# Sliding-window attention into a hard-swish MLP on one core: q and k of the first three batches loaded as fp32 runs in the queue of v and transposed on TensorE, the diagonal ALiBi and mask of two batches added by matmul, weights loaded a slice at a time

## The chip, the core and the metric

One Trainium2 chip, one of its cores. The core has TensorE (PE, matmuls; its weight loads are PEld), VectorE (DVE), ScalarE (ACT), GpSimd (POOL) and SyncE (SP), which run their own instruction streams and meet at semaphores, and 16 DMA engines that move data between device memory and the on-chip SBUF. Matmuls write to PSUM. The metric is the device time of one execution in microseconds (us).

## What is computed

The inputs q, k, v have 8 batches, 8 heads, 576 positions and 64 numbers per head, in fp32. The attention looks back at most 127 positions and adds a bias that falls linearly with the distance (ALiBi); its output, 4608 tokens of 512 numbers, goes through two weight matrices with a hard-swish between them.

```python
    scores = scale * np.matmul(q, k.transpose(0, 1, 3, 2))
    bias = slopes[:, None, None] * (-np.abs(rel).astype(np.float32))[None, :, :]
    mask = (rel >= 0) & (rel < window)          # rel = query position - key position, window = 128
    scores = np.where(mask, scores + bias[None], -1000000000.0)
    ...                                          # softmax over the keys, times v
    h = x @ w_in                                 # x: 4608 x 512, w_in: 512 x 2048
    g = h * np.clip(h + 3.0, 0.0, 6.0) / 6.0
    return (g @ w_out).astype(np.float32)        # w_out: 2048 x 512
```

## The kernel before

**Pairs and slots.** The attention goes over 32 pairs g = 0 to 31; pair g is two heads (e = 0, 1) of batch b = g // 4, with hp = g % 4. The code is written out in order by hand: each engine runs its instructions as they stand, and nothing is reordered. A *slot* g is what one pass of the loop in `first_batch` (g = 0 to 3) or `segment` (g = 4 to 32) issues.

**One pair.** The window is 128, so a block of 128 queries meets its own block of keys (the diagonal, PSUM tile `scd`, five blocks of which the short fifth lies in `sco[448:512]`) and the block before it (off-diagonal, PSUM tile `sco`). `scores` (L203 to L214) makes both on PE with keys on the partitions. `exp_diag` and `exp_off` (L223, L233, L236) take the exponential on ACT into `pd`, `po` and `p4buf`; the ALiBi bias is ACT's bias per partition (`bias_d`, `bias_o`). The causal and window masks are put on afterwards, by `affine_select` on POOL (L226, L242, L246) or, for `po` of batch 0, by a multiplication on DVE (L239). `values` (L263, L266) multiplies with v, whose 65th column of ones gives the softmax sum, and DVE divides (L271, L272) into `avs`. `back` transposes `avs` into `xT`, either on PE with a copy out of PSUM (L292, L294; batches 0 and 1 and pair 31) or by a transposing DMA (L285, `by_xbar`).

**Where q and k come from.** scores needs q and k with the head dimension on the partitions (`qTb`, `kTb`, two buffers each by batch). Batches 0 and 1 are loaded as *runs*: six consecutive tokens of one head are 1536 contiguous bytes, on 96 partitions. These loads go through POOL's DMA queue (L101), which casts to bf16 on the way; `prepare` (L179) reorders a pair, `transposes` (L191, L193) turns it on PE. From batch 2 on q and k are loaded as *tokens* through SP's queue (L110, pieces of 256 bytes), cast by POOL into the one buffer `tbuf` (L164), and turned by a transposing DMA of SP (`xbar`, L169) that takes a whole batch of q or k. v is always loaded as tokens and cast by POOL into `vbuf` (L157, L160). Four load buffers `ldbuf` are handed from tensor to tensor by `slot_of`. The DMAs of SP take turns on eight semaphores, so that each waits for the one issued eight before it.

**The MLP.** 288 *units* follow the attention: `moe_up` (L303, four matmuls of 512 columns, then ACT L307 and DVE L308) and `moe_down` (L320, four matmuls; every fourth one copies out and stores, L332 to L335). A unit of nt (512 tokens) may only run when the batches that it reads are done (`done`). `fill(n)` puts the next n allowed units at its place; the list of seven numbers per slot says how many stand where. Slots 4 to 7 hold four units each, later ones eight. Units of nt = 0 (16) run from slot 4 to slot 8, those that mix nt = 1 with nt = 0 (32) until slot 12, and from slot 13 on 32 units follow each batch; 80 are left after slot 32. Weights come through POOL's queue with a cast to bf16, each matrix in four slices (L138, L144).

## Time and profile before

| | |
|---|---|
| median of 3 runs | 383.64 us (383.27 to 384.53) |
| the profiled execution, its own time | 384.78 us |
| span of its trace, first to last instruction | 383.1 us |
| busy in the span: PE, ACT, DVE, POOL | 319.5, 200.8, 172.6, 152.1 us |

The span is what the rows below add up to; the profiled execution's time is 1.7 us longer than its span and 1.1 us above the median. A share of busy time is a mean over stages that are limited by different things, so the rows are read by stage.

### The profile page before, as it was taken

Reading aid. Unit: us, or ns where it says so; the run is one execution under the profiler, and the core shown is the slowest. Engines: PE = TensorE matmul, PEld = TensorE weight load, DVE = VectorE, ACT = ScalarE, POOL = GpSimd, SP = SyncE. Lnnn points to the kernel's source line nnn. Section 1 sums busy time; section 2 is a strip of 40 time slices with the busy share of each in tenths; the row PEclk is TensorE's granted clock in tenths of the full one; section 3 lists DMA queues with packets and bytes.
Section 4 is the critical chain, followed back from the end, with each engine's and each line's share of the span. In section 5 each row is a group of like instructions: output and inputs, shape, how many; then the busy total and the mean of one; then the engine's idle time right before and its main releaser. Section 6 shows DMA issues by size and latency. Waiting matters only on the chain.

```text
span 383.1 us, 6502 instructions
## 1 busy us (share of the span) xinstructions
PE 319.5 (83%) x2409; PEld 161.6 (42%) x2445; DVE 172.6 (45%) x357; ACT 200.8 (52%) x365; POOL 152.1 (40%) x265
## 2 busy tenths in 40 slices
...
GB/s 169 196 209 204 184 72 68 169 202 216 206 97 230 163 188 113 227 207 161 201 213 240 143 212 220 150 116 72 46 45 47 45 46 38 27 47 36 27 56 82
DMA packets 153135, 51.64 MB, mean 135 GB/s; under 512 B 141200, under 2 KB 148624, under 8 KB 153104
## 3 DMA queue, kind: packets, MB, share of 16 engines
...
q10 hardware_dynamic: 144, 0.13, 0.1%
...
## 4 chain that ended last, share of the span: by engine, by line
PE 57%; issue 6%; DMA 5%; ACT 5%; POOL 4%; SPq 4%; DVE 4%; POOLq 0%
PE ops L320 27%; PE hps L303 24%; SPq L110 4%; DMA xT<-avs 4%; ACT r L307 3%; POOL pd L226 2%; DVE g L308 2%; PE scd L203 2%; PE av L266 1%; POOL tbuf L164 1%; DMA ldbuf<-in_q_dram 1%; PE av L263 1%; DVE osb L334 1%; POOL po L242 1%; PE sco L210 1%
## 5 line engine op out<-in xcount | busy, mean ns | idle before, releaser
L307 ACT ACTIVATE r<-hps,bias 128x512 f32<-128x512 f32 x144 | 99.7, 692 | 132.0 <-PE hps L303 129.6
L308 DVE SCALAR_TENSOR_TENSOR g<-r,hps 128x512 bf16<-128x512 f32 x144 | 99.0, 687 | 148.7 <-ACT r L307 148.6
L303 PE MATMUL hps<-xT,w_in_sb 128*128 128x512 bf16 x553 | 153.1, 394 | 9.9 <-DMA xT<-avs 5.3
L320 PE MATMUL ops<-w_out_sb,g 128*128 128x512 bf16 x563 | 145.1, 382 | 5.7 <-DVE osb L334 3.9
L320 PEld LDWEIGHTS <-g 128*128 128x128 bf16 x576 | 56.0, 98 | 78.6 <-issue 15.0
L303 PEld LDWEIGHTS <-w_in_sb 128*128 128x128 bf16 x576 | 53.3, 101 | 60.4 <-issue 12.5
L226 POOL TENSOR_SCALAR_AFFINE_SELECT pd<-pd 128x512 bf16<-128x512 bf16 x64 | 39.3, 635 | 60.5 <-ACT pd L223 59.4
L164 POOL CAST tbuf<-ldbuf 128x512 bf16<-128x512 f32 (+1 forms) x60 | 34.3, 613 | 46.5 <-issue 32.7
L233 ACT ACTIVATE po<-sco,bias_o 128x512 bf16<-128x512 f32 x64 | 44.4, 694 | 0.0
L242 POOL TENSOR_SCALAR_AFFINE_SELECT po<-po 128x512 bf16<-128x512 bf16 x56 | 35.4, 639 | 20.4 <-ACT po L233 18.0
L223 ACT ACTIVATE pd<-scd,bias_d 128x512 bf16<-128x512 f32 x64 | 41.1, 685 | 2.3 <-PE scd L203 2.3
L266 PE MATMUL av<-vbuf,pd 128*128 128x65 bf16 x248 | 25.2, 203 | 14.1 <-POOL pd L226 14.1
L266 PEld LDWEIGHTS <-pd 128*128 128x128 bf16 x256 | 21.1, 104 | 24.5 <-POOL pd L226 15.3
L272 DVE TENSOR_TENSOR avs<-av,rc 128x384 bf16<-128x384 f32 (+1 forms) x60 | 29.7, 495 | 2.1
L263 PE MATMUL av<-vbuf,po 128*128 128x65 bf16 x240 | 24.5, 200 | 5.2 <-DVE avs L272 3.6
L263 PEld LDWEIGHTS <-po 128*128 128x128 bf16 x256 | 20.8, 104 | 11.0 <-DVE avs L272 5.6
L271 DVE RECIPROCAL rc<-av 128x6 f32<-128x6 f32 (+1 forms) x60 | 11.0, 183 | 25.9 <-PE av L266 25.9
L157 POOL CAST vbuf<-ldbuf 128x1024 bf16<-128x1024 f32 x16 | 16.3, 1043 | 12.9 <-DMA ldbuf<-in_v_dram 12.9
L236 ACT ACTIVATE p4buf<-sco,bias_d 128x64 bf16<-128x64 f32 x64 | 21.0, 329 | 0.0
L332 ACT COPY osb<-ops 128x512 f32<-128x512 f32 x18 | 10.6, 587 | 19.3 <-PE ops L320 19.3
L191 PE MATMUL tp<-ident,pr 96*128 96x96 bf16 x96 | 8.7, 260 | 11.4 <-DVE pr L179 7.9
L292 PE MATMUL tb<-ident,avs 128*128 128x128 bf16 x45 | 7.0, 270 | 11.0 <-DVE avs L272 10.8
...
## 6 DMA issues: line engine op xcount, KB each, us to landing
...
w_in_sb<-in_moe_w_in_dram POOLq DMA_DIRECT2D x4, 512.0 KB, 11.6
w_out_sb<-in_moe_w_out_dram POOLq DMA_DIRECT2D x4, 512.0 KB, 11.9
...
```

The lines of the kernel that those rows point to most:

```text
L164: nc.gpsimd.tensor_copy(out=tbuf[:m, :, j, :], in_=s[:m, j, :, :].rearrange("p (i e) d -> p i (e d)", e=2))
L223: nc.scalar.activation(out=pd[:, e, :, :].rearrange("p j c -> p (j c)"), in_=sc[:, e, :], func=ACT.Exp, bias=bias_d[:, h:h + 1], scale=scale)
L226: nc.gpsimd.affine_select(out=pd[:, e, :, :], in_=pd[:, e, :, :], pattern=[[0, 4], [1, 128]], channel_multiplier=-1, base=0, compare_op=AL ...
L233: nc.scalar.activation(out=po[:, e, :, :].rearrange("p j c -> p (j c)"), in_=sc[:, e, :], func=ACT.Exp, bias=bias_o[:, h:h + 1], scale=scale)
L242: nc.gpsimd.affine_select(out=po[:, e, :, :], in_=po[:, e, :, :], pattern=[[0, 4], [-1, 128]], channel_multiplier=1, base=-1, compare_op=A ...
L263: nc.tensor.matmul(av[:, i, e, :], lhsT=po[:, e, qt - 1, :], rhs=vb[:, qt - 1, h, :], start=True, stop=False)
L266: nc.tensor.matmul(av[:, i, e, :], lhsT=d, rhs=vb[:, qt, h, :], start=(qt == 0), stop=True)
L272: nc.vector.tensor_tensor(out=st[g, "avs"][:, qts[0]:qts[0] + nq, :, :], in0=av[:, 0:nq, :, 0:D], in1=rc[:, 0:nq, :, :].to_broadcast([128, ...
L303: nc.tensor.matmul(hps, lhsT=w_in_sb[:, ks, ts(ms, 128)], rhs=xT[:, ks, ts(nt, NT)], start=(ks == 0), stop=(ks == n_ks - 1))
L307: nc.scalar.activation(out=r6, in_=hps, func=ACT.Relu, bias=bias3[:, 0:1], scale=1.0 / 6.0)
L308: nc.vector.scalar_tensor_tensor(out=gts[nt][:, ms, :], in0=r6, scalar=1.0, in1=hps, op0=ALU.min, op1=ALU.mult)
L320: nc.tensor.matmul(ops[nt, sub], lhsT=gts[nt][:, ms, ts(sub, 128)], rhs=w_out_sb[:, ms, :], start=(ms == 0), stop=(ms == n_ms - 1))
```

## The change

It does nine things.

1. `NB_PE` is 3: q and k of batch 2 too are loaded as runs and transposed on PE, and `back` transposes batch 2 on PE.
2. The runs go through SP's queue (`load_pair`, a pair at a time, fp32 without a cast; the very first k through ACT's queue), in one order with v's tokens: pairs 0 and 1, v of batch 0, pairs 2 and 3, and from there each pair's runs are loaded when `prepare` of the pair four before has read the buffer.
3. `prepare` therefore casts from fp32. For batch 0 q is done on DVE, k on POOL (k of pair 0 on ACT); for batches 1 and 2 both are on POOL.
4. A table `tab` holds, for each head, the ALiBi term by key position and -2^30 (times the slope) where the mask of the diagonal cuts. For batches 0 and 1 (`NB_TAB`) a matmul with the identity puts it into `scd` and `sco[448:512]` first, and q·k is added to it. One exponential of 1024 columns then makes `pd`, one of 128 makes `p4buf`, and POOL's masks on these two are gone in those slots. The mask on `po` is on POOL in all batches.
5. `scores` now issues the short block in `sco` ahead of `scd`.
6. v of batch 0 is cast in slot 1, five pieces on DVE and POOL; the constants are split into what is needed first and later.
7. The weights' eight slices are issued one per slot (slots 1 and 3 to 9).
8. The first loop now runs to slot 4, `back` in it stands one slot later, and the MLP's units begin with two at the end of slot 4; slots 5 to 8 hold 4, 4, 3 and 3 units. Tokens of batch 3 are loaded from slot 4 on.
9. `by_xbar` leaves out the last pair of each batch from batch 3 on, which `back` transposes on PE.

```diff
-    NB_PE = 2
+    NB_PE = 3
+    NB_TAB = 2
...
+    runs = {nm: ldbuf[slot_of(0, nm)][:RP, :].rearrange("p (h c) -> p h c", h=H) for nm in "qk"}
+
+    def load_pair(g, other=None):
+        b, hp = divmod(g, NP)
+        hs = slice(2 * hp, 2 * hp + 2)
+        for nm, eng in (("q", nc.sync), ("k", other or nc.sync)):
+            eng.dma_start(out=runs[nm][:, hs, :],
+                          in_=src_of[nm][b, hs, :, :].rearrange("h (p t) d -> p h (t d)", t=RT))
...
+        base_i, base_b = base[:, 0:128].bitcast(INT32), base[:, 256:320].bitcast(BF16)
+        nc.gpsimd.iota(base_i, pattern=[[0, 128]], base=-64, channel_multiplier=1)
+        nc.gpsimd.tensor_copy(out=base_b, in_=base_i)
+        nc.gpsimd.affine_select(out=base_b, in_=base_b, pattern=[[1, 128]],
+                                channel_multiplier=-1, base=0,
+                                compare_op=ALU.is_ge, fill=-(2.0 ** 30))
+        for h in range(H):
+            nc.vector.tensor_scalar(out=tab[:, h, :], in0=base_b, scalar1=slopes[h] / scale,
+                                    scalar2=0.0, op0=ALU.mult, op1=ALU.add)
...
+    def load_w_in(g):
+        nc.gpsimd.dma_start(
+            out=w_in_sb[:, :, ts(g, 512)],
+            in_=moe_w_in[:, ts(g, 512)].rearrange("(k p) f -> p k f", p=128))
...
+    def cast_v(b, j, eng):
+        n = min(128, S - j * 128)
+        eng.tensor_copy(out=vbuf[b % 2][:n, j, :, 0:D], in_=ld[b, "v"][:n, j, :, :])
...
-        for nm, eng in (("q", nc.vector), ("k", nc.gpsimd if 2 <= g < NP else nc.vector)):
+        for nm in "qk":
             pr = prs.tile([RP, RT, 2, D], BF16, tag=f"pr{nm}", name="pr")
-            eng.tensor_copy(
-                out=pr.rearrange("p t e d -> p e t d"),
-                in_=ld[b, nm][:, hs, :].rearrange("p e (t d) -> p e t d", t=RT))
+            if g == 0 and nm == "k":
+                copy = nc.scalar.copy
+            elif nm == "q" and g < NP:
+                copy = nc.vector.tensor_copy
+            else:
+                copy = nc.gpsimd.tensor_copy
+            copy(out=pr.rearrange("p t e d -> p e t d"),
+                 in_=runs[nm][:, hs, :].rearrange("p e (t d) -> p e t d", t=RT))
             st[g, nm] = pr
+        if g + NP < NB_PE * NP:
+            load_pair(g + NP)
...
+        first = not tabled(g)
         scd = ps_sc.tile([128, 2, 512], FP32, tag="sc", name="scd")
+        sco = ps_sc.tile([128, 2, 512], FP32, tag="sc", name="sco")
+        if tabled(g):
+            for e in range(2):
+                t = tab[:, 2 * hp + e:2 * hp + e + 1, :]
+                nc.tensor.matmul(scd[:, e, :].rearrange("p (j c) -> p j c", j=4), lhsT=ident,
+                                 rhs=t.to_broadcast([128, 4, 128]), start=True, stop=False)
+            for e in range(2):
+                nc.tensor.matmul(sco[:, e, 448:512], lhsT=ident,
+                                 rhs=tab[:, 2 * hp + e, 0:64], start=True, stop=False)
+        for e in range(2):
+            r = slice(e * D, (e + 1) * D)
+            nc.tensor.matmul(sco[:, e, 448:512], lhsT=kT[r, 4, :],
+                             rhs=qT[r, 4, 0:LAST], start=first, stop=True)
         for j in range(4):
...
                 nc.tensor.matmul(scd[:, e, ts(j, 128)], lhsT=kT[r, j, :],
-                                 rhs=qT[r, j, :], start=True, stop=True)
-        sco = ps_sc.tile([128, 2, 512], FP32, tag="sc", name="sco")
+                                 rhs=qT[r, j, :], start=first, stop=first or j == 3)
...
+        if tabled(g):
+            if e == 0:
+                nc.scalar.activation(out=pd.rearrange("p e j c -> p e (j c)"), in_=sc,
+                                     func=ACT.Exp, scale=scale)
+            return
...
+        if tabled(g):
+            if e == 1:
+                nc.scalar.activation(out=p4[:, :, 0:64], in_=sc[:, :, 448:512],
+                                     func=ACT.Exp, scale=scale)
+            return
...
-        if g < NP:
-            nc.vector.tensor_tensor(out=po[:, e, :, :], in0=po[:, e, :, :],
-                                    in1=mask_off.to_broadcast([128, 4, 128]), op=ALU.mult)
-        else:
-            nc.gpsimd.affine_select(out=po[:, e, :, :], in_=po[:, e, :, :],
-                                    pattern=[[0, 4], [-1, 128]], channel_multiplier=1, base=-1,
-                                    compare_op=ALU.is_ge, fill=0.0)
...
     def by_xbar(g):
-        return XBAR_X and 2 * NP <= g < G - 1
+        return XBAR_X and g >= NB_PE * NP and g % NP < NP - 1
...
+        if g < 10:
+            slices = {1: (load_w_in, 0), 3: (load_w_in, 1), 4: (load_w_in, 2), 5: (load_w_in, 3),
+                      6: (load_w_out, 0), 7: (load_w_out, 1), 8: (load_w_out, 2),
+                      9: (load_w_out, 3)}
+            if g in slices:
+                fn, n = slices[g]
+                fn(n)
+        if g == 4:
+            cast_tokens(1, "v")
+            load_tokens(3, "q")
+        if g == 7:
+            cast_tokens(2, "v")
+            load_tokens(3, "k")
+        if g == 8:
+            cast_tokens(3, "q")
+        if g == 9:
             load_tokens(3, "v")
-        if b >= 2 and b + 1 < B:
+            xbar(3, "q")
+            cast_tokens(3, "k")
+        if g == 10:
+            xbar(3, "k")
+            load_tokens(4, "q")
+        if g == 11:
+            cast_tokens(3, "v")
+            load_tokens(4, "k")
+            load_tokens(4, "v")
+            cast_tokens(4, "q")
...
     def first_batch():
...
         for g in range(NP + 1):
+            scores(g)
+            exp_diag(g, 0)
+            exp_diag(g, 1)
+            transposes(g + 1)
+            if g == 1:
+                cast_v(0, 0, nc.vector)
+                cast_v(0, 1, nc.vector)
+                cast_v(0, 2, nc.gpsimd)
+            exp_off(g, 0)
+            exp_off(g, 1)
+            if g == 1:
+                cast_v(0, 3, nc.vector)
+                cast_v(0, 4, nc.gpsimd)
             if g > 0:
                 values(g - 1, (0, 1, 2))
                 values(g - 1, (3, 4))
+            if g > 1:
+                back(g - 2)
+            prepare(g + 2)
+            if g == 2:
+                load_tokens(2, "v")
+                more_constants()
+            if g == NP:
                 back(g - 1)
...
+            stage_next(g)
+
+    FILLS = {5: (1, 1, 0, 1, 0, 1, 0), 6: (1, 1, 0, 1, 0, 1, 0),
+             7: (1, 0, 1, 0, 1, 0, 0), 8: (1, 0, 1, 0, 1, 0, 0)}
 
...
+        load_pair(0, nc.scalar)
+        load_pair(1)
         load_tokens(0, "v")
+        load_pair(2)
+        load_pair(3)
...
         prepare(0)
-        cast_tokens(0, "v")
-        new_runs(1)
         first_batch()
...
+        fill(2)
+        segment(NP + 1, G, lambda g: FILLS.get(g, (1, 1, 1, 1, 1, 1, 2)))
         done[0] = G
         fill(len(units))
```

**The order on SP.** SP issues the loads. These are the first rows of its queue before: v of batches 0 and 1, then q of batch 2 as tokens (`ldbuf0` to `ldbuf3` are the load buffers; DMAHW are the eight semaphores of SP's own DMAs, DMASW those of POOL's).

```order
L110 DMA ldbuf1_103<-in_v_dram 128x8x64 x4
L110 DMA ldbuf1_103<-in_v_dram 64x8x64
L110 DMA ldbuf0_102<-in_v_dram 128x8x64 [waits DMASW2_49,DMASW0_49,DVE_49]
L110 DMA ldbuf0_102<-in_v_dram 128x8x64 [waits DMASW4_49,DVE_49]
L110 DMA ldbuf0_102<-in_v_dram 128x8x64 [waits DMASW6_49,DVE_49]
L110 DMA ldbuf0_102<-in_v_dram 128x8x64 [waits DMAHW0_49,DMASW3_49,DMASW1_49]
L110 DMA ldbuf0_102<-in_v_dram 64x8x64 [waits DMAHW1_49,DMASW5_49,Pool_49]
L110 DMA ldbuf1_103<-in_q_dram 128x8x64 [waits DMAHW2_49]
```

And the first rows of the same queue in the change.

```order
L99 DMA ldbuf0_103<-in_q_dram 96x2x384 x2
L99 DMA ldbuf2_105<-in_k_dram 96x2x384
L107 DMA ldbuf1_104<-in_v_dram 128x8x64 x4
L107 DMA ldbuf1_104<-in_v_dram 64x8x64 [waits DMAHW0_49]
L99 DMA ldbuf0_103<-in_q_dram 96x2x384 [waits DMAHW1_49]
L99 DMA ldbuf2_105<-in_k_dram 96x2x384 [waits DMAHW2_49]
L99 DMA ldbuf0_103<-in_q_dram 96x2x384 [waits DMAHW3_49]
L99 DMA ldbuf2_105<-in_k_dram 96x2x384 [waits DMAHW4_49]
L99 DMA ldbuf0_103<-in_q_dram 96x2x384 [waits DMAHW5_49,DVE_49]
L99 DMA ldbuf2_105<-in_k_dram 96x2x384 [waits DMAHW6_49,Activation_49]
L99 DMA ldbuf0_103<-in_q_dram 96x2x384 [waits DMAHW7_49,DVE_49]
L99 DMA ldbuf2_105<-in_k_dram 96x2x384 [waits DMAHW0_49,Pool_49]
```

The eight runs of batch 0 that stood in POOL's queue now share SP's with v, and the first loads of batch 1 (the last four rows) wait for the casts of pairs 0 and 1.

**The order on POOL.** POOL casts and masks in one stream. Before, from the end of slot 6: the four slices of `w_out`, the masks of pair 7, the casts of v of batch 2 and of q of batch 3, and behind them the masks of pair 8 (the last row is the first of these).

```order
L144 DMA w_out_sb<-in_moe_w_out_dram 128x4x512 x4
L226 AFFINE_SELECT pd<-pd 128x512 x2
L242 AFFINE_SELECT po<-po 128x512 x2
L246 AFFINE_SELECT p4buf_110<-p4buf_110 128x2x64
L157 CAST vbuf_106<-ldbuf_104 128x16x64 x2
L160 CAST vbuf_106<-ldbuf_104 64x8x64
L164 CAST tbuf<-ldbuf_102 128x4x128 x4
L164 CAST tbuf<-ldbuf_102 64x4x128
L226 AFFINE_SELECT pd<-pd 128x512 x2
```

In the change, from the end of slot 7: one slice, v of batch 2, the masks of pair 8, `prepare` of pair 10, one slice, q of batch 3, and then the masks of pair 9.

```order
L153 DMA w_out_sb<-in_moe_w_out_dram 128x4x512
L165 CAST vbuf_107<-ldbuf_104 128x16x64 x2
L168 CAST vbuf_107<-ldbuf_104 64x8x64
L258 AFFINE_SELECT pd<-pd 128x512 x2
L268 AFFINE_SELECT po<-po 128x512 x2
L279 AFFINE_SELECT p4buf_109<-p4buf_109 128x2x64
L193 CAST pr<-ldbuf_103 96x2x6x64
L193 CAST pr<-ldbuf_105 96x2x6x64
L153 DMA w_out_sb<-in_moe_w_out_dram 128x4x512
L172 CAST tbuf<-ldbuf_106 128x4x128 x4
L172 CAST tbuf<-ldbuf_106 64x4x128
L258 AFFINE_SELECT pd<-pd 128x512 x2
```

The masks of pair 8 now stand ahead of the cast of q of batch 3, whose tokens SP was given in slot 4 (L172 is the old L164, L165 and L168 are L157 and L160, L258, L268 and L279 the masks, L193 is `prepare`).

## Rows read from the trace of the kernel before

**Rows 1.** Stretches of the span: from, to, length; busy us per engine; PEclk, DMA share, GB/s.

```profile
0.00:45.59 45.59, 24.58 (x273) 17.35 (x274) 25.91 (x75) 20.84 (x40) 23.11 (x43) 1.00 1.14 195
45.59:82.14 36.55, 26.52 (x241) 13.90 (x244) 19.84 (x41) 22.15 (x43) 20.51 (x35) 0.81 0.71 121
82.14:135.94 53.80, 35.36 (x257) 16.52 (x260) 15.50 (x32) 21.36 (x40) 27.15 (x46) 0.84 1.09 185
135.94:148.26 12.32, 9.70 (x69) 4.69 (x70) 4.07 (x9) 5.36 (x10) 4.71 (x9) 0.86 0.57 128
148.26:290.26 142.00, 137.83 (x1140) 69.74 (x1157) 71.69 (x145) 96.49 (x179) 73.91 (x129) 1.00 0.83 160
290.26:383.10 92.84, 85.56 (x435) 39.35 (x443) 35.59 (x58) 34.58 (x54) 2.75 (x5) 0.99 0.12 45
```

**Rows 2.** Timeline of PE, first score matmuls of slots 0, 2, 3, 14 and 15.

```profile
9.78 0.61 PE L203 MATMUL scd<-qTb,kTb 64*128 64x128 bf16 x8 [0.73 <-ACT kTb L193]
...
22.48 0.61 PE L203 MATMUL scd<-qTb,kTb 64*128 64x128 bf16 x8
...
27.90 0.61 PE L203 MATMUL scd<-qTb,kTb 64*128 64x128 bf16 x8
...
148.26 0.40 PE L203 MATMUL scd<-qTb,kTb 64*128 64x128 bf16 x8
...
156.37 0.40 PE L203 MATMUL scd<-qTb,kTb 64*128 64x128 bf16 x8
```

**Rows 3.** Timeline of PE, the long waits between 82 and 180 us.

```profile
93.55 0.23 PE L266 MATMUL av<-vbuf,pd 128*128 128x65 bf16 x1 [8.82 <-POOL pd L226]
...
110.23 0.24 PE L266 MATMUL av<-vbuf,pd 128*128 128x65 bf16 x1 [4.53 <-POOL pd L226]
...
139.72 0.59 PE L303 MATMUL hps<-xT,w_in_sb 128*128 128x512 bf16 x1 [2.40 <-DMA xT<-avs]
...
175.76 0.38 PE L303 MATMUL hps<-xT,w_in_sb 128*128 128x512 bf16 x1 [1.79 <-DMA xT<-avs]
```

**Rows 4.** Timeline of POOL, its two longest waits for a DMA in a cast.

```profile
83.80 1.04 POOL L157 CAST vbuf<-ldbuf 128x1024 bf16<-128x1024 f32 x1 [9.99 <-DMA ldbuf<-in_v_dram]
...
106.74 2.84 POOL L164 CAST tbuf<-ldbuf 128x512 bf16<-128x512 f32 x5 [11.24 <-DMA qTb<-tbuf]
```

**Rows 5.** Timeline of PE: the end of slot 6, and units back to back after the attention.

```profile
62.42 0.20 PE L263 MATMUL av<-vbuf,po 128*128 128x65 bf16 x1 [0.83 <-DVE avs L272]
...
64.21 0.29 PE L292 MATMUL tb<-ident,avs 128*128 128x128 bf16 x2 [1.21 <-DVE avs L272]
64.33 1.64 PE L303 MATMUL hps<-xT,w_in_sb 128*128 128x512 bf16 x4
...
310.52 1.03 PE L303 MATMUL hps<-xT,w_in_sb 128*128 128x512 bf16 x4
311.38 1.03 PE L320 MATMUL ops<-w_out_sb,g 128*128 128x512 bf16 x4
```

**Rows 6.** Groups by line and shape, whole span: count, then busy us and mean ns.

```profile
L223 ACT ACTIVATE pd<-scd,bias_d 128x512 bf16<-128x512 f32 x64 | 41.1, 685 | 2.3 <-PE scd L203 2.3
L164 POOL CAST tbuf<-ldbuf 128x512 bf16<-128x512 f32 x48 | 27.6, 614 | 46.2 <-issue 32.7 <-DMA qTb<-tbuf 11.2 <-DMA ldbuf<-in_q_dram 1.9
L179 DVE COPY pr<-ldbuf 96x768 bf16<-96x768 bf16 x14 | 6.3, 469 | 2.7 <-DMA ldbuf<-in_k_dram 1.7 <-DMA ldbuf<-in_q_dram 1.0
L179 POOL COPY pr<-ldbuf 96x768 bf16<-96x768 bf16 x2 | 1.8, 908 | 0.0
```

**Rows 7.** DMA: five token loads on SP; queues from 0 to 45 us (packets, MB, share); w_in.

```profile
112.60 4.35 SPq L110 DMA_DIRECT2D ldbuf<-in_q_dram  x5
...
q0 software_dynamic: 5344, 4.46, 62.0%
q1 hardware_dynamic: 17037, 4.29, 51.9%
...
w_in_sb<-in_moe_w_in_dram POOLq DMA_DIRECT2D x4, 512.0 KB, 11.6
```

More of the change, by code (lines that the diff above doesn't have):

```diff
@@ L57 @@
     warm = perm.tile([128, 1], FP32)
+    tab = perm.tile([128, H, 128], BF16)
     rel_i = perm.tile([128, 1], INT32)
@@ L194, in transposes, with tabled @@
                 "p (a t) -> p a t", t=RT), in_=tp.rearrange("p t a -> p a t"))
+    def tabled(g):
+        return g < NB_TAB * NP
     def scores(g):
@@ L211, in scores @@
                                  rhs=qT[r, j + 1, 0:n], start=True, stop=True)
-        for e in range(2):
-            r = slice(e * D, (e + 1) * D)
-            nc.tensor.matmul(sco[:, e, 448:512], lhsT=kT[r, 4, :],
-                             rhs=qT[r, 4, 0:LAST], start=True, stop=True)
         st[g, "scd"], st[g, "sco"] = scd, sco
@@ L387, in stage_next @@
                 cast_tokens(b + 1, "kkv"[hp])
-        if b >= 2 and b + 2 < B:
+        if b >= 3 and b + 2 < B:
             if hp > 0:
@@ L396, in first_batch @@
         prepare(1)
+        load_tokens(1, "v")
+        biases()
         for g in range(NP + 1):
-            if g < NP:
-                scores(g)
-                exp_diag(g, 0)
-                exp_diag(g, 1)
-            if g + 1 < NP:
-                transposes(g + 1)
-            if g < NP:
-                exp_off(g, 0)
-                exp_off(g, 1)
+            scores(g)
[11 more added lines that the diff above has]
+                cast_v(0, 4, nc.gpsimd)
             if g > 0:
```

115 lines of the change are left out of this document (31 added, 84 removed).

## The prediction

> **What bounds the kernel now.** Read the stretches first [rows 1]. Units back to back start 0.86 us apart [rows 5], so a 512-column matmul takes 0.215 us and 288 units of four take 248 us: PE is the bound wherever it is busy. From 148 us on it is, 137.8 us of 142.0. Before that it isn't: PE is busy 24.6 of the first 45.6 us, 26.5 of the next 36.6, 35.4 of the next 53.8, and 9.7 of the 12.3 of slot 13, at a granted clock of 0.81 to 0.86 in the last three. These early stretches hold 148 us, of which 52 are idle PE, and this is what the change can win. What comes after slot 13 is nearly fixed: 240 units and 19 pairs of attention.
>
> Next, what PE waits for in each stretch. Between slots 9 and 13 it waits 8.82 us and 4.53 us for POOL's mask of `pd` [rows 3]. POOL was not slow: it stood 9.99 us in the cast of v of batch 2 for the load, and 11.24 us in the cast of k of batch 3 until the transposing DMA had emptied `tbuf` [rows 4]; the masks are queued behind these casts. In slots 5 to 8 the waits are short, 0.83 us and 1.21 us for DVE's `avs` in slot 6 and nearly the same in 5 and 7, but after them the four matmuls of a unit take 1.64 us instead of 0.86 [rows 5]: PE has dropped from its 2.4 to its 1.2 GHz level. In the first batch PE is at the 1.2 GHz level as well, though the granted clock reads 1.00 there: eight score matmuls take 0.61 us, 0.40 in slot 14 [rows 2].
>
> **The sum** goes by these stretches, from the profile's span of 383.1 us.
>
> *A, to the start of slot 5: 45.6 us before.* The first scores start at 9.78 us [rows 2]. In the change q and k of pair 0 no longer wait for POOL, which issues its DMAs one after another; I put the first scores at 8. Slots 2 and 3 were 5.4 us apart [rows 2], because `back` of the pair before stood in the same slot behind masks and DVE. In the change its input is a slot old, and the two masks on `pd` and `p4buf` are gone. The table adds 2 x 512 + 2 x 64 = 1152 columns, 0.48 us at 0.215 us per 512 and 0.97 at half the clock. PE's work in such a slot at the 1.2 GHz level is then about 4.5 us: 18 score matmuls 1.0 (at most 1.2, twice the columns of the eight that take 0.61 with the last one's end), the table 0.97, twelve transposes 0.97 (1152 columns), 18 value matmuls 1.0 (1170 columns), `back` 0.54 (640 columns). That is also near ACT's chain: 1.2 us for `pd` (two of 685 ns, overlapping) [rows 6], 1.2 for `po`, a copy of 0.6, and the gap until the next scores, since `sco`, now filled first, must be free before the rest of the slot's scores. I take 4.6 us for slots 2 to 4, and 17 us for the start of slot 2, because slot 1 waits for v: v stands behind pairs 0 and 1, so it lands near 10 us, the casts of its five pieces take some 3 us more, then values and DVE. Slot 5's start follows: 17 + 3 x 4.6, and 5 for the last `back`, its copy and two units, makes 36. **A: -9.6.** Bounds: 31, if PE reaches 2.4 GHz in slot 2; 45.6, if the loads arrive no sooner.
>
> Do they? From 0 to 45 us a packet of POOL's queue took 0.62 x 16 x 45 us / 5344 = 84 ns and one of SP's queue, mostly 256 bytes, 0.519 x 16 x 45 / 17037 = 22 ns [rows 7]. A run of 1536 bytes is nearest to POOL's packets. So q and k of a batch (1536 packets) cost 8 us over 16 engines, and v (4608) 6.3; batch 0 is 14 us of DMA, pair 3 last, which slot 2 needs near 16. The shares add up to 1.14 [rows 1], so little is in reserve. Five loads of at most 256 KB each were issued in 4.35 us [rows 7], so pieces overlap in a queue, and the runs should too. The Trainium skill, "DMA: Bandwidth & Descriptors", section Bandwidth, part Measured, speaks against it: it wants 1 MiB or more in each DMA, and a run load is 288 KiB. By its fit of 2.0 us plus bytes at 436 GB/s (in the section on the anatomy of one DMA), an estimate, eight such loads one after another with v between them would put pair 3 near 26 us, slot 2 some 9 us later and the sum at 361; by the row it is 352.
>
> *B, slots 5 to 8: 36.6 us before.* Both kernels run 14 units here. Added: `transposes` of two more pairs (slots 7 and 8), 0.7 us each between the two clock levels; the table in slots 5 to 7, also 0.7 each. Removed: the 1.21 us wait for DVE in slots 7 and 8, where a unit now stands ahead of `back`, and one stretch of slow units, 0.8. That is +1.4 + 2.1 - 2.4 - 0.8 = +0.3. POOL does two casts in `prepare`, by the 614 ns for 512 columns [rows 6] 0.92 us each; with `po`'s masks and a DMA issue that is under 4 us of a 9 us slot, v's cast in slots 4 and 7 2.6 more, so it hides. The same copy took 908 ns on POOL and 469 on DVE [rows 6], so 19 casts would add 8.3 us if POOL were on the path. The Trainium skill, "GPSIMD Engine Reference", section Engine selection, gives elementwise work to VectorE; by that rule the move costs, up to 360, by the time POOL has left it costs nothing. **B: +0.3**, so slot 9 starts at 73. Bounds: 26, if PE holds 2.4 GHz throughout (14 units 12.1, attention with both transposes 4 x 2.0, table 1.5, and 1.1 a slot for the waits that stay); 43, if all of it (14 units, attention, table) runs at half the clock.
>
> *C, slots 9 to 12: 53.8 us before with 29 units, now 32*, since slot 8 leaves three more. A steady slot with eight units is 8.1 us [rows 2]. Four are 32.4; added are four `back` on PE at 0.27 and two `transposes` at 0.5, and 2.5 for slot 9, where eight `moe_up` follow each other and share two PSUM buffers. **C: 37.3, -16.5.** This rests on the waits of 8.82 and 4.53 us going. The first goes: batch 3's tokens are asked for four slots ahead, and the masks of pair 8 stand before the cast. The second keeps its mechanism: in slot 9 the cast of k of batch 3 waits for the transposing DMA of q. But only the last token load of v now precedes that DMA. In the order of the change it is issued about when slot 10 starts; cast and masks of pair 10 follow some 10 us later, and `values` of pair 10 wants them 11 us into it. Bounds: 35; 48, if both waits return in part.
>
> *D, slot 13 to the end: 247.2 us before.* Slot 13 falls from 12.3 us to 8.1: its wait of 2.40 us for the transposing DMA of `xT`, with the slow clock behind it, has gone, because batch 2 is transposed on PE. Later waits of this kind, 1.79 us [rows 3] and smaller ones, sum to about 3.5 between 148 and 290 us (142.0 against 17 x 8.11 = 137.9, less a little for others); they fall on the last pair of a batch, which PE now does for 4 x 0.27, taken as 1.4 with its copy. **D: -4.2 - 3.5 + 1.4 = -6.3.** Bounds -3 and -8.
>
> Sum: -9.6 + 0.3 - 16.5 - 6.3 = -32, a span of 351. With 1.7 us beside the span the profiled execution takes 352.8, and 1.1 less is the median: **352 us**.
>
> **Rivals.**
> 1. *The forecast*, 344 to 360: 0.50.
> 2. *PE holds its 2.4 GHz level from slot 2 on.* For it: fewer waits on POOL, `back` a slot later. Against: the waits for `avs` in slots 5 and 6 stay. A and B end near their low bounds, -5 and -8 to -10: about 339. 0.18.
> 3. *The wait for `tbuf` returns in slot 10*, as at 110 us: 4.5 us, PE at 1.2 GHz for some 2 us of work behind it, and a late slot 12 or 13, in all 8 to 12: 360 to 364. 0.14.
> 4. *The change doesn't do what it says at the start*: fp32 runs in one FIFO, with v between them, land no sooner than POOL's casting loads did beside v, A stays at 45.6: 361. For it: the shares that already add up to 1.14. Against: the 4.35 us for five loads. 0.12. (The small-load rule of "DMA: Bandwidth & Descriptors" in the Trainium skill ends here.)
> 5. *Slower: the weights come late.* A slice is issued at the end of a slot and its first unit stands in the next but one. If landing takes longer than two slots, every slot from 5 to 10 stretches to half of it. Landing took 11.6 us in the median [rows 7]; the shortest time left, for the second slice, is about 12, the others have 16. To lose the 32 us over six slots each must grow by 5.3, to 13.5, so a slice would have to land after 27 us. 0.04. The rest, 0.02, is no change.
>
> **How the numbers follow.** The prediction is the first case. The range of 8 in 10 reaches from case 2 to past cases 3 and 4: 339 to 369. What counts as no change is 0.3%, about what a measurement of this kernel can tell. Cases 1 to 4 are faster (0.94), 0.02 the same, 0.04 slower.
>
> **What would show it.** Right: scores of slot 5 near 36 us, of slot 9 near 73, of slot 13 near 110; no wait of PE for `pd` above 3 us; POOL's cast of batch 2's v without a wait; `xT` by DMA no longer ahead of a wait of PE; 241 us from slot 13 to the end. Wrong: slot 2 later than 20 us (the loads), score matmuls of slots 3 to 8 at the 2.4 GHz level (case 2), a POOL cast with a long wait on qTb followed by PE waiting on `pd` (case 3), `hps` waiting on `w_in_sb` (case 5).

## The result, and the profile after

The changed kernel takes 365.39 us (364.52 to 365.71, four runs) against 383.86 for the kernel before (383.27 to 384.53): a ratio of 0.9515, interval 0.9491 to 0.9538. It is faster, and 13 us above the forecast of 352. Its profiled execution took 365.52 us with a span of 363.8.

The same view as [rows 1], for the stretches of the forecast in the kernel after (start to slot 5, slots 5 to 8, 9 to 12, slot 13, the rest in two):

```profile
0.00:38.09 38.09, 20.86 (x287) 14.80 (x290) 21.05 (x65) 18.80 (x31) 22.02 (x41) 0.82 1.11 224
38.09:70.82 32.73, 24.65 (x276) 14.14 (x279) 18.51 (x37) 20.58 (x37) 15.84 (x24) 0.95 1.09 204
70.82:114.45 43.63, 36.85 (x312) 18.87 (x320) 20.53 (x41) 24.45 (x45) 26.91 (x46) 1.00 1.08 181
114.45:129.48 15.03, 10.86 (x70) 4.96 (x72) 4.10 (x9) 5.47 (x10) 5.44 (x10) 0.77 0.65 144
129.48:279.41 149.93, 147.00 (x1224) 74.53 (x1246) 77.67 (x158) 101.85 (x189) 75.97 (x132) 1.00 0.76 149
279.41:363.80 84.39, 77.46 (x368) 35.04 (x373) 31.05 (x49) 29.21 (x44) 0.00 (x0) 1.00 0.12 44
```

| stretch | before | forecast | after | error |
|---|---|---|---|---|
| A, to slot 5 | 45.6 | 36 | 38.1 | +2.1 |
| B, slots 5 to 8 | 36.6 | 36.9 | 32.7 | -4.2 |
| C, slots 9 to 12 | 53.8 | 37.3 | 43.6 | +6.3 |
| D, slot 13 to the end | 247.2 | 241 | 249.4 | +8.4 |
| span | 383.1 | 351.2 | 363.8 | +12.6 |

Three places explain A, C and D. The first is the start of slot 2. The timeline of all engines in slot 1 (SPq is SP's DMA queue, its number the time taken by the issue):

```profile
2.24 7.51 SPq L107 DMA_DIRECT2D ldbuf<-in_v_dram  x5
9.79 0.61 SPq L99 DMA_DIRECT2D ldbuf<-in_q_dram  x1
...
14.79 0.56 DVE L193 CAST pr<-ldbuf 96x768 bf16<-96x768 f32 x1 [3.81 <-DMA ldbuf<-in_q_dram]
...
15.40 0.66 PE L206 MATMUL tp<-ident,pr 96*128 96x96 bf16 x6 [3.64 <-DVE pr L193]
...
18.95 0.27 PE L299 MATMUL av<-vbuf,pd 128*128 128x65 bf16 x2 [1.35 <-DVE vbuf L159]
...
22.39 0.62 PE L235 MATMUL scd<-qTb,kTb 64*128 64x128 bf16 x8
```

The five token loads of v stand ahead of pair 2's q on SP's queue and take SP 7.51 us to issue; q is issued only at 9.79, and PE waits 3.64 us for its cast. The casts of v come behind that on DVE. So slot 2 starts at 22.39 instead of the 17 forecast.

The late issue need not be what delayed it. The pieces on SP's queue landed in the order of issue, from 6.6 to 25.2 us one every 1.05 to 1.35 us: the last of v at 13.68, q of pair 2 next, at 14.76. The DMA engines are busy nine tenths or more of every microsecond from 3 us on (one digit a microsecond, in tenths):

```profile
DMA  0179999999999999999999999999999999999999
```

The second is slot 9, which took 14.08 us. PE's timeline:

```profile
73.62 1.89 PE L336 MATMUL hps<-xT,w_in_sb 128*128 128x512 bf16 x7
...
76.14 2.18 PE L336 MATMUL hps<-xT,w_in_sb 128*128 128x512 bf16 x8 [0.33 <-DVE g L341]
...
81.38 1.89 PE L336 MATMUL hps<-xT,w_in_sb 128*128 128x512 bf16 x8 [0.52 <-DVE g L341]
83.90 1.02 PE L336 MATMUL hps<-xT,w_in_sb 128*128 128x512 bf16 x3 [0.63 <-DVE g L341]
...
84.90 0.22 PE L235 MATMUL scd<-qTb,kTb 64*128 64x128 bf16 x1
```

Eight `moe_up` units, with the value matmuls and `back` of pair 8 between them, fill 73.62 to 84.90. These 11.3 us are 1.41 us a unit, where PE needs 0.86 [rows 5] and some 0.1 for its share of the rest, and PE waits for DVE's `g`: in the code a buffer of `ps_h` is free again only when ACT and DVE have read it.

The third is slot 13, 15.03 us long at a granted clock of 0.77. All engines:

```profile
108.77 6.98 SPq L107 DMA_DIRECT2D ldbuf<-in_v_dram  x5
115.85 1.04 SPq L368 DMA_DIRECT2D out_dram<-osb  x2
...
119.22 0.69 DVE L367 COPY osb<-ops 128x512 f32<-128x512 f32 x1 [6.83 <-DMA out_dram<-osb]
...
119.96 1.86 PE L353 MATMUL ops<-w_out_sb,g 128*128 128x512 bf16 x4 [3.95 <-DVE osb L367]
...
123.88 1.91 PE L353 MATMUL ops<-w_out_sb,g 128*128 128x512 bf16 x4
```

Two stores of `osb` stand behind the token loads of v of batch 4 on SP's queue: the last piece of v landed at 118.47, the first store at 119.12. `opool` has two buffers, so DVE's copy waits 6.83 us for a store to land, PE 3.95 us for that copy, and then four matmuls take 1.86 and 1.91 us: PE is at its 1.2 GHz level.

What was forecast right: no wait of PE for `pd` above 3 us, where [rows 3] had 8.82 and 4.53. POOL's cast of v of batch 2 has no wait for the load, but its cast of k of batch 3 still waits as in [rows 4]:

```profile
65.87 2.03 POOL L165 CAST vbuf<-ldbuf 128x1024 bf16<-128x1024 f32 x2
...
92.30 2.84 POOL L172 CAST tbuf<-ldbuf 128x512 bf16<-128x512 f32 x5 [9.28 <-DMA qTb<-tbuf]
95.11 1.22 POOL L258 TENSOR_SCALAR_AFFINE_SELECT pd<-pd 128x512 bf16<-128x512 bf16 x2
```

The second cast is half of the sign of rival 3; the other half, PE waiting on `pd`, is missing, since the masks came in time.

### The profile page after: what moved, and what is told of

Same layout as the page of the kernel before. It is cut to its first block, busy times and chain, and to the rows that moved or that the text cites. A ratio compares the mean times of both kernels' runs of the same rounds, so it can differ in the third digit from the quotient of the medians.

```text
span 363.8 us, 6702 instructions
## 1 busy us (share of the span) xinstructions
PE 317.7 (87%) x2523; PEld 162.3 (45%) x2565; DVE 172.9 (48%) x357; ACT 200.4 (55%) x354; POOL 146.2 (40%) x251
## 4 chain that ended last, share of the span: by engine, by line
PE 62%; ACT 8%; SPq 7%; DVE 7%; issue 5%; POOL 5%; DMA 5%; POOLq 0%; DVEq 0%
PE hps L336 27%; PE ops L353 26%; SPq L107 6%; ACT r L340 3%; DMA qTb<-tbuf 3%; ACT po L265 2%; DVE g L341 2%; POOL pd L258 2%; POOL pr L193 2%; PE scd L235 1%; PE av L299 1%; DMA ldbuf<-in_q_dram 1%; PE tp L206 1%; PE sco L241 1%; DVE osb L367 1%
## 5 line engine op out<-in xcount | busy, mean ns | idle before, releaser
L336 PE MATMUL hps<-xT,w_in_sb 128*128 128x512 bf16 x545 | 146.8, 384 | 8.2 <-DVE g L341 5.0
L268 POOL TENSOR_SCALAR_AFFINE_SELECT po<-po 128x512 bf16<-128x512 bf16 x64 | 40.1, 635 | 41.9 <-ACT po L265 39.3
L258 POOL TENSOR_SCALAR_AFFINE_SELECT pd<-pd 128x512 bf16<-128x512 bf16 x48 | 29.4, 635 | 42.5 <-ACT pd L255 42.5
L172 POOL CAST tbuf<-ldbuf 128x512 bf16<-128x512 f32 (+1 forms) x50 | 28.4, 613 | 37.8 <-issue 28.5
L255 ACT ACTIVATE pd<-scd,bias_d 128x512 bf16<-128x512 f32 x48 | 30.3, 684 | 0.6 <-PE scd L235 0.6
L299 PE MATMUL av<-vbuf,pd 128*128 128x65 bf16 x248 | 22.8, 196 | 2.5 <-DVE vbuf L159 2.5
L299 PEld LDWEIGHTS <-pd 128*128 128x128 bf16 x256 | 19.6, 99 | 11.7 <-issue 2.7
L296 PEld LDWEIGHTS <-po 128*128 128x128 bf16 x256 | 19.3, 100 | 10.7 <-DVE avs L305 6.5
L193 POOL CAST pr<-ldbuf 96x768 bf16<-96x768 f32 x19 | 15.2, 821 | 8.6 <-PE tp L206 4.6
L367 DVE COPY osb<-ops 128x512 f32<-128x512 f32 x17 | 11.6, 685 | 14.0 <-PE ops L353 7.2
L276 ACT ACTIVATE p4buf<-sco,bias_d 128x64 bf16<-128x64 f32 x48 | 15.6, 325 | 0.0
L206 PEld LDWEIGHTS <-pr 96*128 96x128 bf16 x144 | 7.9, 108 | 16.9 <-DVE pr L193 9.5
```

Of the source, the lines that this page charges most:

```text
L172: nc.gpsimd.tensor_copy(out=tbuf[:m, :, j, :], in_=s[:m, j, :, :].rearrange("p (i e) d -> p i (e d)", e=2))
L255: nc.scalar.activation(out=pd[:, e, :, :].rearrange("p j c -> p (j c)"), in_=sc[:, e, :], func=ACT.Exp, bias=bias_d[:, h:h + 1], scale=scale)
L258: nc.gpsimd.affine_select(out=pd[:, e, :, :], in_=pd[:, e, :, :], pattern=[[0, 4], [1, 128]], channel_multiplier=-1, base=0, compare_op=AL ...
L268: nc.gpsimd.affine_select(out=po[:, e, :, :], in_=po[:, e, :, :], pattern=[[0, 4], [-1, 128]], channel_multiplier=1, base=-1, compare_op=A ...
L296: nc.tensor.matmul(av[:, i, e, :], lhsT=po[:, e, qt - 1, :], rhs=vb[:, qt - 1, h, :], start=True, stop=False)
L299: nc.tensor.matmul(av[:, i, e, :], lhsT=d, rhs=vb[:, qt, h, :], start=(qt == 0), stop=True)
```

## The experiments

All are edits of the changed kernel, timed against the kernel before. "Slot n took" is the time between the first `scd` score matmuls of slots n and n+1. Runs are compared with each other by their ratios to the kernel before (0.01 is 3.8 us), since that kernel took 383.9 to 385.5 us beside them; the changed kernel's ratio is 0.9515. Slots 0 to 8 differ between executions of identical code: slot 9 starts at 70.8 in the kernel after and at 69.3 in run 3, which touches nothing before slot 15; it starts at 71.2 in run 5 and at 68.6 in run 9, which have the same code to the end of slot 10. So a difference under 3 us in A and B together is not read as an effect.

**1. v of batch 4 one slot later.**

```diff
         if g == 11: ...
-            load_tokens(4, "v")
+        if g == 12:
+            load_tokens(4, "v")
```

> Edit: the five token loads of v of batch 4 are issued one slot later (slot 12, behind the transposing DMA of q of batch 4); nothing else. Theory S (slot 13 took 15.0 us because a store of `osb` stood behind these loads on SP's queue, and DVE's copy of the next `osb` and PE's `ops` waited for that store): the 3.95 us wait of PE for `osb` is gone, slot 13 takes 8 to 10 us, the span falls by 5 to 7 us (ratio to the kernel before about 0.935 to 0.940). Rival R (two `osb` buffers are too few for eight moe_down units in a row, whatever stands ahead on the queue): the wait moves to another store of slots 12 to 14, the span changes by less than 2 us.

358.5 us, ratio 0.9305 (0.9257 to 0.9353). Slot 13 took 8.1 us, the span is 7.3 shorter. SP's queue now:

```profile
108.24 2.31 SPq L368 DMA_DIRECT2D out_dram<-osb  x2
110.66 3.87 SPq L177 DMA_TRANSPOSE qTb<-tbuf  x1
114.58 4.37 SPq L107 DMA_DIRECT2D ldbuf<-in_v_dram  x5
```

The same two stores are issued at 108.24 instead of 115.85. Theory S holds: with two buffers as before the stall is gone, so it was what stood ahead of the stores. (Runs 4 and 5 remove it by another order of the units, with v left in place: it takes both the loads ahead and two stores close together.)

**2. No table.**

```diff
-    NB_TAB = 2
+    NB_TAB = 0
```

(`bias_d` is then filled ahead of slot 0.)

> Edit: the table of ALiBi and mask is not used (number of tabled batches 0); batches 0 and 1 take bias_d in the Exp and three masks on POOL, as the later batches do. Theory T (the table is paid by PE and bought off POOL, and PE had no wait for `pd` in slots 0 to 7 that POOL could not have hidden): stretch A within 1 us of 38.1, stretch B 1 to 2 us shorter than 32.7, since PE saves some 0.6 us in slots 4 to 7, in all -1 to -2 us. Rival P (without it POOL, with the casts of pair k and q and v in the same slots, becomes late with `pd`): PE waits for POOL `pd` by 1 us or more in slots 1 to 7, and the span grows by 3 to 8 us.

369.9 us, 0.9601 (0.9560 to 0.9641), slower than the changed kernel by 0.0086, some 3 us (span 366.5 against 363.8). Neither theory as written: slot 4 took 10.4 us (8.8 with the table, 7.6 to 9.2 in the other runs with the same code there), and slot 10 starts at 89.0 (84.9). Slot 9 took 15.3 (14.1), but so it did in run 3, where its code is unchanged. PE does not wait for masks of `pd` there, but for POOL's casts behind them, 2.3 us in slot 4 (0.7 with the table):

```profile
32.22 0.62 PE L206 MATMUL tp<-ident,pr 96*128 96x96 bf16 x6 [2.15 <-POOL pr L193]
```

The table pays; that it does so by what it takes off POOL ahead of the casts is read from these waits.

**3. The last pair of a batch by DMA again.**

```diff
-        return XBAR_X and g >= NB_PE * NP and g % NP < NP - 1
+        return XBAR_X and NB_PE * NP <= g < G - 1
```

> Edit: from batch 3 on the last pair of a batch too goes into `xT` by transposing DMA, as in the kernel before (only the very last pair by PE); batch 2 stays on PE. Theory G (the prediction's 3.5 us of waits for that DMA are real and are what PE's `back` replaces; but `back` with its copy in the path costs 0.98 us in each of slots 16, 20, 24 and 28): the four slots take about 8.1 us, the waits of 0.5 to 1.8 us for `xT` return in the slots behind, the span changes by less than 1.5 us. Rival N (the waits came from how SP's queue stood in the kernel before, and do not return): the span falls by 3 to 4 us.

364.8 us, 0.9468 (0.9433 to 0.9503), span 363.5 against 363.8. The four slots 16, 20, 24 and 28 take 8.1 us instead of 9.1, and slots 17, 21 and 25 take 9.2, 9.7 and 10.1 instead of 8.1. PE's waits from 129 us on:

```profile
PE hps L336 <- DMA xT<-avs: 4.2, 3, 1.8
```

Theory G: the DMA waits were real, and `back` on PE costs as much.

**4. Row tile 1 nearly in turn.**

```diff
-    units += [(1, moe_up, step) for step in range(8)]
-    for step in range(8):
-        units += [(1, moe_up, 8 + step), (1, moe_down, step)]
-    units += [(1, moe_down, 8 + step) for step in range(8)]
+    units += [(1, moe_up, step) for step in range(4)]
+    for step in range(12):
+        units += [(1, moe_up, 4 + step), (1, moe_down, step)]
+    units += [(1, moe_down, 12 + step) for step in range(4)]
```

> Edit: order of the units of row tile 1 alone: 4 moe_up, then 12 pairs of moe_up and moe_down, then 4 moe_down, instead of 8, 8 pairs, 8; the number of units in each slot stays. Theory U (slot 9 took 14.1 us because eight moe_up in a row share two PSUM buffers with the transposes, and each must pass ACT and DVE before its buffer is free): slot 9 falls to 10 to 11 us, the waits for DVE's `g` of 0.3 to 0.6 us go; the eight moe_down in a row of slots 12 and 13 are fewer too, so the store that comes late in slot 13 comes late by less; in all -4 to -8 us. Rival M (slot 9 is long because POOL's casts of the last pair and the load of k keep PE waiting, or because slots 10 to 12 take back what slot 9 gives): slots 9 to 12 together stay within 1.5 us of 43.6.

363.5 us, 0.9436 (0.9399 to 0.9472). Slot 9 took 12.6, but slot 10 13.8: its fourth `moe_down` meets a slice of w_out that has not landed.

```profile
90.75 1.02 PE L353 MATMUL ops<-w_out_sb,g 128*128 128x512 bf16 x4 [2.37 <-DMA w_out_sb<-in_moe_w_out_dram]
```

Inconclusive by itself; slot 13 fell to 8.1 here as well, and slot 14 took 10.1.

**5. Row tile 1 in turn, w_out two slices a slot.** In the unit list the lines for row tile 1 (those that 4 changes) go and the common loop starts at row tile 1, and

```diff
-                      6: (load_w_out, 0), 7: (load_w_out, 1), 8: (load_w_out, 2),
-                      9: (load_w_out, 3)}
+                      6: (load_w_out, 0), 7: (load_w_out, 2)}
...
+                if g > 5:
+                    fn(n + 1)
```

> Edit: row tile 1 is worked off like every later one, moe_up and moe_down in turn from slot 9 on, and the four slices of w_out are issued two by two, in slots 6 and 7 instead of 6 to 9, so that all are there by slot 9 (the run with only the units changed waited 2.37 us for the fourth slice, and its slot 9 fell only from 14.1 to 12.6 us). Theory U (moe_up units in a row are paced by their two PSUM buffers: in slot 9 of the changed kernel eight of them start at 73.6 us and end at 84.9, 1.41 us each, where PE needs 0.86): slot 9 takes 10 to 11 us, slot 10 about 10, slot 13 8 to 9 because no eight moe_down stand in a row there and the store of `osb` has more time; the span falls by 6 to 11 us. Rival M (slot 9 is long because of what else ACT, DVE and POOL do in it): slots 9 to 12 stay within 2 us of 43.6, and only slot 13 gains.

358.95 us, 0.9330 (0.9292 to 0.9368). Slots 9 to 12 took 11.6, 10.3, 9.1 and 9.1, together 40.1; slot 13 8.1. PE in slot 9 has one wait of 0.44 us for `g` left. Theory U holds for most of the slot; 1.5 us of waits for POOL's casts stay. New is slot 14 with 10.8 us: q's transposing DMA of batch 4 stands behind v's token loads, POOL's cast behind that DMA, and the masks behind the cast. POOL's and PE's timeline:

```profile
119.34 2.83 POOL L172 CAST tbuf<-ldbuf 128x512 bf16<-128x512 f32 x5 [10.44 <-issue]
...
122.81 0.20 PE L299 MATMUL av<-vbuf,pd 128*128 128x65 bf16 x1 [0.92 <-POOL pd L258]
```

**6. Pair 2 ahead of v of batch 0.**

```diff
-        load_tokens(0, "v")
         load_pair(2)
+        load_tokens(0, "v")
```

> Edit: the four... two run loads of pair 2 are issued ahead of the five token loads of v of batch 0 on SP's queue instead of behind them; nothing else. Theory F (in stretch A PE waits 3.64 us for q of pair 2, which stands behind v's token loads, 7.5 us of issue on SP): that wait is gone, slot 2 starts at 18 to 20 us instead of 22.4, v lands about 1 us later and the wait for `vbuf` stays at 2 to 3 us; the span falls by 2 to 4 us. Rival V (v is as late, and slot 1 needs it: the wait only changes its name): slot 2 starts at 21.5 to 23, the span changes by less than 1 us.

363.7 us, 0.9450 (0.9409 to 0.9490): 1.0 us less by the span, 2.5 by the ratio. Slot 2 starts at 17.55, as the forecast had it, and slot 5 at 35.2, but slot 9 at 69.8: slots 5 and 6 took 10.1 and 10.0 us. The stretches of slots 2 and 3, of slot 4 and of slot 5 (columns as above):

```profile
17.55:25.18 7.63, 7.36 (x117) 5.95 (x118) 5.34 (x20) 5.57 (x10) 5.77 (x9) 0.70 1.21 243
25.18:35.21 10.03, 7.33 (x74) 4.07 (x74) 3.42 (x10) 5.83 (x10) 4.87 (x8) 0.69 1.11 228
35.21:45.28 10.07, 8.12 (x76) 4.34 (x77) 5.06 (x11) 5.41 (x9) 7.40 (x10) 0.84 1.24 233
```

The granted clock is 0.70, 0.69 and 0.84, where the kernel after has 0.93, 0.81 and 1.00 in the same slots. Run 9, with the kernel after's order of loads, has 0.75 in slots 2 and 3 and 1.00 in slot 4, so the order isn't shown to be the reason.

**7. Run loads on POOL's queue.**

```diff
-        for nm, eng in (("q", nc.sync), ("k", other or nc.sync)):
+        for nm, eng in (("q", nc.gpsimd), ("k", nc.gpsimd)):
```

> Edit: the run loads of q and k (all twelve pairs, still fp32 and still cast on chip) are issued on POOL's DMA queue instead of SP's (k of pair 0: ACT's). Theory H (the shared HWDGE queue is what brings the first pairs early): eight issues of about 0.87 us on POOL stand ahead of `ident`, first scores at 11 to 14 us instead of 7.9, and slots 0 to 7 lose 0.9 us of POOL each; stretch A 3 to 5 us longer, the span 3 to 6 us. Rival Q (the queue order on SP costs more than POOL's issue does: pairs 2 and 3 no longer stand behind v's token loads): slot 2 no later than 22.4 us, the span within 2 us of 363.8 or shorter.

(The very first k goes with them.) 370.65 us, 0.9628 (0.9580 to 0.9677), slower than the changed kernel by 0.0113, some 4 us (span 367.1 against 363.8). First scores at 12.4 us instead of 7.9, slot 2 at 25.3. Theory H in size; the issues took 0.64 us each, and in the first 40 us the run loads land 8.7 (q) and 9.1 us (k) after their issue in the median, 6.2 and 6.9 on SP's.

**8. v of batch 2 late.**

```diff
             if g == 2:
-                load_tokens(2, "v")
...
         if g == 7:
+            load_tokens(2, "v")
             cast_tokens(2, "v")
```

> Edit: the token loads of v of batch 2 are issued in slot 7, right ahead of their cast on POOL, as late against the cast as in the kernel before, instead of in slot 2. Theory L (the 16 us that stretch C had to win came from this load's place: POOL stood in the cast and the masks of `pd` stood behind it): POOL waits 7 to 10 us in the cast at 66 us, the masks of pair 8 come at 75 to 78, PE waits 2 to 6 us for POOL in slots 8 to 10; the span grows by 3 to 10 us. Rival K (the win is due to other parts: batch 2 on the transposing path of PE, the weights): POOL's wait hides, the span grows by less than 1.5 us.

364.1 us, 0.9451 (0.9406 to 0.9496), span 363.4. Slot 10 starts at 88.1 us (84.9), by a wait in another place than expected. PE in slot 9:

```profile
73.64 1.43 PE L206 MATMUL tp<-ident,pr 96*128 96x96 bf16 x12 [4.52 <-POOL pr L193]
75.15 3.57 PE L336 MATMUL hps<-xT,w_in_sb 128*128 128x512 bf16 x8
```

POOL waits 4.0 us for v in the cast, its casts of the next pair come after that, PE waits 4.52 us for them and then runs eight matmuls in 3.57 us, at the 1.2 GHz level. Given back: slot 13 took 11.4 us instead of 15.0. So theory L holds for the place, not for the engine's operand, and the total hides it as K would; the load's place is worth 3 us at the start of slot 10, and 5.5 within slot 9 (19.6 against 14.1).

**9. Edits 1 and 5 together**, from the kernel of 5:

```diff
-            load_tokens(4, "v")
...
+        if g == 12:
+            load_tokens(4, "v")
```

> Edit: the two edits that gained, together: v of batch 4 loaded in slot 12, and row tile 1 worked off in turn with w_out's slices in slots 6 and 7. Theory A (each removes a wait of its own): slots 9 to 12 as with the turn alone (11.6, 10.3, 9.1, 9.1), slot 13 8.1, and slot 14 8.1 instead of the 10.8 of the turn alone, since q's transposing DMA no longer stands behind v's token loads and POOL's masks of pair 14 behind it; span 353 to 355, ratio 0.922 to 0.928. Rival B (both edits take away the same stall of slot 13, and the 2.7 us of slot 14 have another cause): span 356 to 357, ratio 0.930 to 0.934.

355.7 us, 0.9237 (0.9206 to 0.9268). Slots 9 to 12 took 11.6, 10.3, 9.7 and 9.1, slots 13 and 14 8.1 each. Theory A. Its slot 13 in the view of [rows 1]:

```profile
109.33:117.45 8.12, 8.12 (x71) 4.07 (x72) 4.53 (x10) 5.36 (x10) 5.42 (x10) 1.00 1.18 239
```

**10. Edits 1, 5 and 6 together**, from the kernel of 9:

```diff
-        load_tokens(0, "v")
         load_pair(2)
+        load_tokens(0, "v")
```

> Edit: the former kernel with pair 2's run loads ahead of v's token loads. Alone, that edit brought slot 2 forward from 22.4 to 17.6 us, and slot 9 only from 70.8 to 69.8, with a granted clock of 0.70 and 0.69 in slots 2 to 4 and 0.84 in 5 and 6. Theory C (what is won at the start is given back because PE then runs these slots at its 1.2 GHz level): slot 2 at 17 to 18 us, slot 9 within 1.5 us of the kernel without this edit, the clock of slots 2 to 6 lower than there. Rival N (the low clock was chance of one execution): clock about the same, slot 9 3 to 5 us earlier, ratio lower by 0.008 to 0.013.

354.4 us, 0.9190 (0.9154 to 0.9227): the fastest median here, though its interval overlaps that of 9 and its profiled span is no shorter (352.8 against 351.8). Slot 5 starts 4.0 us earlier than in 9 and slot 9 at the same time, 68.6. The clock is not the reason in this execution (slots 5 to 8 at 0.95): theory C falls, and the earlier slot 9 of rival N doesn't come either. Slot 5 took 12.7 us, because the run of pair 6 is not there: it was issued at 27.98 and landed at 35.25, in its turn on the queue. POOL's cast and PE's transpose:

```profile
35.30 0.82 POOL L193 CAST pr<-ldbuf 96x768 bf16<-96x768 f32 x1 [4.97 <-DMA ldbuf<-in_q_dram]
...
36.18 0.43 PE L206 MATMUL tp<-ident,pr 96*128 96x96 bf16 x6 [2.36 <-POOL pr L193]
```

**11. Weights in bursts.**

```diff
-            slices = {1: (load_w_in, 0), 3: (load_w_in, 1), ...
+        bursts = {0: (load_w_in, 0, 2), 1: (load_w_in, 2, 4), 6: (load_w_out, 0, 4)}
```

> Edit, to the changed kernel alone: the weights in bursts, two slices of w_in in each of slots 0 and 1 and four of w_out in slot 6, in place of one slice in a slot (1, 3 to 9). Theory W (the DMA share is above 1 up to slot 8, so four weight slices among the first loads delay pairs 2 to 5 and v of batches 0 and 1): slot 2 or slot 5 3 to 8 us later, the span 2 to 6 us longer. Rival E (the loads of each pair have slots of slack, and w_out, all there by slot 9, costs nothing): slot 5 within 1.5 us of 38.1, the span within 1.5 us of 363.8.

364.65 us, 0.9468 (0.9441 to 0.9494): no loss in the total, but slot 2 starts 1.7 us later, slot 5 takes 13.2 us (8.5) and slot 9 starts at 76.0 (70.8). It comes back because slot 13 takes 8.8 instead of 15.0. Theory W up to slot 9; the end hides it. One slice a slot is worth some 5 us ahead of slot 9, less the 3 that executions differ by.

**12. Edits 1 and 5, and the table for batch 2**, from the kernel of 9:

```diff
-    NB_TAB = 2
+    NB_TAB = 3
```

> Edit: the kernel with both edits, and the table of ALiBi and mask for batch 2 too (slots 8 to 11). Theory P (in these slots PE hardly waits for POOL's masks, so the table only adds 1152 columns, 0.48 to 0.6 us a slot): slots 8 to 11 together 1.5 to 2.5 us longer, the span 1 to 2.5 us longer than that of the kernel with both edits. Rival Q (POOL's two masks of `pd` gone let its casts of the last pairs and of q and k of batch 3 come earlier, and PE waited 1.3 to 1.5 us for these in slot 9): slot 9 1 us shorter, the span the same or up to 1.5 us shorter.

356.2 us, 0.9250 (0.9220 to 0.9279), the same as 9. Slots 8 to 11 took 7.2, 10.8, 10.7 and 9.9, with 7.5, 11.6, 10.3 and 9.7 in 9: slot 9 gains what slots 10 and 11 pay, and neither theory's change of the total is seen.

## Why the prediction was right in sign and short in size

The time lies in the stated range, 339 to 369 us, but outside the 344 to 360 of the first case; that it falls near the 360 to 364 of rival 3 and the 361 of rival 4 is chance, since PE did not wait for `pd` and A did fall.

**A, +2.1.** The failed step is "slot 2 at 17, because slot 1 waits for v". v, put near 10 us, landed at 13.68, and it was the second wait; the first was pair 2, which stood behind v on the queue. The order of loads on SP was not followed past pairs 0 and 1. With pair 2 first the start is 17.55 (run 6). The 4.6 us for slots 2 and 3 was too much (3.3 and 3.6 at a clock of 0.93), so that A came out near is luck: 5.4 too little for slot 2, 3.1 too much for slots 2 to 4. The 4.35 us for five token loads [rows 7] was a row from 112 us on; in the stretch that was forecast, SP of the kernel before needed more:

```profile
30.23 8.73 SPq L110 DMA_DIRECT2D ldbuf<-in_q_dram  x5
39.00 6.48 SPq L110 DMA_DIRECT2D ldbuf<-in_k_dram  x5
```

A took 38.1 and not 45.6, and loads in SP's queue land earlier than in POOL's (run 7), so rival 4 is out; no wait of PE for a weight slice is among its long ones, so rival 5 is too. The rule of the Trainium skill, "DMA: Bandwidth & Descriptors", section Bandwidth, part Measured, asks for 1 MiB in a DMA, and its fit, in the section on the anatomy of one DMA, is of loads issued from GpSimd. The forecast's estimate from them, slot 2 near 26, isn't borne out by the 22.39 here and the 17.55 of run 6. By the fit one run load takes 2.7 us, an estimate; here one landed every 1.1 to 1.2 us between 14.8 and 22.9 us.

**B, -4.2.** The sum counted slow PE at the 0.81 of [rows 1]; the clock was 0.95, and 1.00 in run 9 (31.3 us). Waits of PE for `avs` still make 5.5 us in the stretch (six, at most 1.2 each), 2.1 of them in slots 7 and 8, where the sum counted them as gone. Rival 2 came partly true, here alone.

**C, +6.3.** The main step, that PE's waits for `pd` go, is right: 53.8 to 43.6 with three units more. The terms of the sum add up to 37.0, not to the 37.3 written. Two of them were mis-sized. "2.5 for slot 9" measured some 5: slot 9 took 14.08, against 8.1 and 0.77 for transposes and `back`; run 5 gives 2.5 of it back. And `back` on PE at 0.27 a slot measured 0.98: slot 11, with nothing else new, took 9.08 against 8.11. Slots 10 and 12 took 1.2 and 0.6 more than this explains. In the code `back` takes one of the two `ps_h` buffers from `moe_up`; no run gave it another, so this cause is argued. In slot 16, PE behind `back`:

```profile
151.10 0.53 PE L325 MATMUL tb<-ident,avs 128*128 128x128 bf16 x5
151.47 1.03 PE L353 MATMUL ops<-w_out_sb,g 128*128 128x512 bf16 x4
152.94 1.02 PE L336 MATMUL hps<-xT,w_in_sb 128*128 128x512 bf16 x4 [0.44 <-DVE g L341]
```

The Trainium skill, "GPSIMD Engine Reference", section Engine selection, gives elementwise add, mul and max to VectorE; it puts GpSimd at about half the speed for two inputs and roughly at line-rate for one, which is what a cast has. Here a cast of a pair's q or k takes 821 ns on POOL and 551 on DVE. The forecast put the casts' cost on POOL at nothing; PE waits for them 4.6 us in all, 1.3 of it in slot 9. No run moved them to VectorE, so what that would give isn't shown.

**D, +8.4.** The failed step is "slot 13 falls to 8.1: its wait for the transposing DMA has gone". That wait did go, and another took its place: +6.9 (run 1). It could be read from the order: two token loads, k and v, were put into slot 11 on the queue that also carries the stores. The other term, 1.4 for four `back`, measured 3.9 (4 x 0.98), and run 3 shows that it just pays for the 4.2 us of waits that it removes. 6.9 + 2.5 is 9.4, near the error of 8.4.

**What carried the gain of 19.3 us of span**: A -7.5, B -3.8, C -10.2, D +2.2. Of single parts, undone alone, the run loads on SP are worth some 4 us (run 7) and the table some 3 (run 2); the earlier load of v of batch 2 and the single slices are worth something up to slots 9 and 10 but not in the total, because the late store of slot 13 takes in what is won before it. With the losses of slots 9 and 13 edited away (runs 9 and 10) the kernel takes 355.7 and 354.4 us, 2 to 4 above the forecast, so the rest of the sum held in total, if not in its parts.

Left open: why the clock in slots 2 to 8 is granted so differently after nearly the same waits, and whether the DMA engines bound much of A and B. For it: the DMA share is 1.1 to 1.2, SP's pieces land in order at an even pace, the start of slot 9 hardly moves when slot 2 or 5 comes earlier (runs 6 and 10), and the gain in A goes with the rate of the transfers (224 GB/s, 195 in [rows 1]), for which the forecast's sum has no term. Against it: in slot 5 of run 6 PE was busy 8.1 of 10.1 us at a clock of 0.84. No run took load bytes away.
